# Turning the query order of the exponentials, so that one DMA stores a unit's result, in a hashed-attention and feed-forward kernel

## The chip, the cores and the metric

The kernel runs on one core of a Trainium2 chip. The metric is the device time of one execution in microseconds (us). Single executions of the same kernel scatter by up to 1.6% here (the kernel before: 303.5 to 308.3 us over its fast runs), so differences of less than that are read from several rounds and an interval, never from one run. One run of the kernel before, 308.87 us, counted as slow and is left out. One profiled execution of each kernel gives the trace.

TensorE does the matmuls, ScalarE the exponentials, VectorE and GpSimd other work on elements, and SyncE (SP) issues most transfers. SBUF is the working memory on the chip, PSUM the memory into which the matmuls write their sums. The granted clock is the share of its full clock that TensorE was given.

## The reference

```python
# attention over (4, 8, 768, 64): only pairs in the same hash bucket count
q_bucket, k_bucket = bits(q @ proj > 0), bits(k @ proj > 0)          # 6 bits
scores = where(q_bucket == k_bucket, q @ k.T / sqrt(64), -1e9)
attn = softmax(scores)
x = (attn @ v) as (batch, seq, 8 * 64)
# feed-forward on rows of x
xn = (x - mean) / sqrt(var + 1e-6) * g_ln
out = x + relu(xn @ w_ch1) @ w_ch2                                   # 512 -> 2048 -> 512
# [cut: shapes, the drawing of the inputs]
```

## The kernel before

The work goes in 12 units of 256 queries, three to a batch. A unit has six steps; a step makes scores (four heads, 256 keys, 256 queries) on TensorE into two PSUM tiles, two exponentials on ScalarE take them to bf16 in SBUF, and later matmuls use these tiles as weights against the values. The order of every instruction on every engine is fixed by one long word list.

```python
KJ, CC, TT = 6, 4, 32
out_view = [out[b].rearrange("(tt c u qt) d -> u c tt qt d", tt=TT, c=CC, u=3) for b in range(B)]

def S_(eng, s, h):        # scores: 24 matmuls a step, into two PSUM tiles [128, 2, 512] fp32
    # [cut]

def E_(eng, s, h):        # two of these a step; E is [128, 4, 512] bf16 in SBUF
    nc.scalar.activation(E(s)[:, heads(h)], sc(s, h), AF.Exp, scale=EXP_SCALE, bias=bias_sb)

def A_(eng, s, h):        # E as weights: 128 adjacent columns become 128 output partitions
    # [cut: loops]
    nc.tensor.matmul(acc[...], E(s)[:, i, 256 * kk + P * qt : 256 * kk + P * qt + P], vaug(...), ...)

def O_(eng, u, *a):       # the result of unit u: x is [128, 2, 512] fp32
    # [cut: which t, c, half]
    eng.dma_start(
        out=out_view[u // 3][u % 3][c][:, t, half(h)], in_=xt(u)[32 * c : 32 * c + 32, t, half(h)],
    )
```

A block of 128 queries lies in the order (c, t), c of 4 and t of 32, because the transposes on VectorE (L246, 72 of them in the trace), with the views of the kernel's `turn`, leave it so. The result therefore has partition 32c + t, while the row in DRAM goes with 4t + c, and a unit needs four stores of 32 partitions.

The softmax here doesn't subtract the row's maximum and nothing guards it: scores larger than these inputs give would overflow.

Of the kernel before, what the change touches and what calls it, by code (L numbers as in the profile page):

```python
# [590 lines left out]
```

## Time and profile before

| Kernel before | value |
|---|---|
| time, first three runs | 304.38, 305.44, 308.29 us |
| span of the profiled run | 303.0 us |
| TensorE busy | 292.2 us, 96% |
| ScalarE busy | 194.6 us, 64%, of it 153.1 us in 144 exponentials |
| stores | 56 (50 on SP's queue, 6 on ACT's) |

The lines themselves stand in the prediction. They are to be read from the busiest engine outwards: TensorE is nearly never idle (192.32 of 195.00 us busy from 75 to 270 us), ScalarE waits for TensorE (39.9 us for scores there), and the stores hold a queue for which no wait of TensorE is listed there.

### The profile page before, as it was taken

Reading aid. Unit: us, or ns where it says so; the run is one execution under the profiler, and the core shown is the slowest. Engines: PE = TensorE matmul, PEld = TensorE weight load, DVE = VectorE, ACT = ScalarE, POOL = GpSimd, SP = SyncE. Lnnn points to the kernel's source line nnn. Section 1 sums busy time; section 2 is a strip of 40 time slices with the busy share of each in tenths; the row PEclk is TensorE's granted clock in tenths of the full one; section 3 lists DMA queues with packets and bytes.
Section 4 is the critical chain, followed back from the end, with each engine's and each line's share of the span. In section 5 each row is a group of like instructions: output and inputs, shape, how many; then the busy total and the mean of one; then the engine's idle time right before and its main releaser. Section 6 shows DMA issues by size and latency. Waiting matters only on the chain.

```text
span 303.0 us, 9838 instructions
## 1 busy us (share of the span) xinstructions
PE 292.2 (96%) x4319; PEld 204.8 (68%) x4360; DVE 169.7 (56%) x348; ACT 194.6 (64%) x215; POOL 72.0 (24%) x112
## 2 busy tenths in 40 slices
PE   8999899999999999999999999999999999999994
PEld 7667676676666667676667677776657667685673
DVE  4678878378258527766345767555217446266012
ACT  2977789667667788686567676557666767561320
POOL 2792500211771005041600520911000101001000
PEclk9999999999999999999999999999999999999999
DMA  6999996937255265516306100310502102403122
GB/s 202 381 340 306 209 205 142 268 111 169 47 147 122 61 217 167 94 74 160 73 2 175 38 8 8 75 42 19 89 2 71 37 2 19 105 4 74 30 71 69
DMA packets 30426, 33.58 MB, mean 111 GB/s; under 512 B 15536, under 2 KB 27056, under 8 KB 30384
## 3 DMA queue, kind: packets, MB, share of 16 engines
...
HBM read 27.53 MB, written 6.29 MB: 112 GB/s over the span
## 4 chain that ended last, share of the span: by engine, by line
PE 80%; DMA 6%; SPq 6%; DVE 3%; issue 2%; ACT 1%; DVEq 0%; ACTq 0%
PE f L511 26%; PE sc L443 15%; PE acc L458 10%; DMA X<-in_q_dram 4%; SPq L420 3%; PE hp L408 3%; DMA xnT<-xc 3%; ACT E L449 1%; SPq L294 1%; PE f_100None L527 1%; PE f_101None L527 1%; PE f L527 1%; PE f_11None L527 1%; PE f_51None L527 1%; PE f_80None L527 1%
## 5 line engine op out<-in xcount | busy, mean ns | idle before, releaser
L449 ACT ACTIVATE E<-sc,bias_sb 128x1024 bf16<-128x1024 f32 x144 | 153.1, 1111 | 49.5 <-PE sc L443 48.3
L511 PE MATMUL f<-xnT,w_sb 128*128 128x256 bf16 x768 | 99.3, 273 | 0.8 <-DMA xnT<-xc 0.7
L511 PEld LDWEIGHTS <-w_sb 128*128 128x128 bf16 x768 | 70.9, 98 | 23.5 <-issue 7.9
L519 ACT ACTIVATE hb<-f 128x512 bf16<-128x512 f32 x57 | 33.9, 597 | 44.6 <-PE f L511 44.5
L527 PEld LDWEIGHTS <-hb 128*128 128x128 bf16 x400 | 37.7, 98 | 34.5 <-issue 2.7
L521 DVE TENSOR_SCALAR hb<-f 128x512 bf16<-128x512 f32 x39 | 26.9, 690 | 46.7 <-PE f L511 46.4
L443 PE MATMUL sc<-qb,kb 32*128 32x256 bf16 x1152 | 52.2, 267 | 0.0
L458 PEld LDWEIGHTS <-E 128*128 128x128 bf16 x1152 | 40.0, 98 | 6.5 <-issue 3.8
L458 PE MATMUL acc<-vaug,E 128*128 128x65 bf16 x1152 | 43.4, 194 | 0.1
L443 PE MATMUL sc<-G 6*128 6x256 bf16 x576 | 41.7, 273 | 0.9 <-DVE G L249 0.3
L489 POOL TENSOR_SCALAR rs<-mv 128x2 f32<-128x2 f32 x12 | 7.1, 595 | 104.6 <-DVE mv L483 104.3
L443 PEld LDWEIGHTS <-kb 32*128 32x128 bf16 x1152 | 30.2, 93 | 1.6
L443 PEld LDWEIGHTS <-G 6*128 6x128 bf16 x576 | 15.2, 91 | 18.8 <-issue 15.6
L246 DVE STREAM_TRANSPOSE T<-X 128x384 f32<-128x384 f32 x48 | 24.8, 554 | 3.4 <-PE hp L408 1.4
L469 DVE SCALAR_TENSOR_TENSOR acc<-vsB,acc 128x520 f32<-128x520 f32 x24 | 16.8, 701 | 15.3 <-PE acc L458 15.0
L356 POOL TENSOR_TENSOR t<-vn 128x256 f32<-128x256 f32 x18 | 12.9, 727 | 35.0 <-DMA out_dram<-x 18.0
L346 POOL CAST vaug<-vn 128x768 bf16<-128x768 f32 x16 | 13.1, 831 | 25.9 <-DMA G<-B 12.7
L484 DVE SCALAR_TENSOR_TENSOR xc<-x,mv,gB 128x512 bf16<-128x512 f32 x24 | 18.6, 776 | 0.8
L480 DVE BATCH_NORM_STATS2 st<-x 128x6 f32<-128x256 f32 x48 | 18.0, 417 | 0.7
L476 DVE TENSOR_TENSOR x<-acc,rc 128x512 f32<-128x512 f32 x24 | 16.6, 691 | 0.8
L257 POOL CAST kb<-T 128x768 bf16<-128x768 f32 x10 | 8.4, 842 | 30.2 <-DVE T L246 30.2
L315 PE MATMUL hf<-tp,pfull 128*128 128x256 f32 x48 | 13.2, 401 | 0.6 <-DVE tp L246 0.5
...
## 6 DMA issues: line engine op xcount, KB each, us to landing
...
G<-B SPq DMA_DIRECT2D x96, 4.5 KB
...
```

The lines of the kernel that those rows point to most:

```text
L246: nc.vector.transpose(d[:, j], s[:, j, kj0 : kj0 + n])
L443: nc.tensor.matmul(sc(s, i // 2)[:, i % 2, 256 * kk : 256 * kk + 256], lh, rh, start=(rep == 0), stop=(rep == 2), skip_group_check=True,)
L449: nc.scalar.activation(E(s)[:, heads(h)], sc(s, h), AF.Exp, scale=EXP_SCALE, bias=bias_sb)
L458: nc.tensor.matmul(acc[:, qt, (D + 1) * i : (D + 1) * (i + 1)], E(s)[:, i, 256 * kk + P * qt : 256 * kk + P * qt + P], vaug(u // 3)[:, 4 * ...
L469: nc.vector.scalar_tensor_tensor(acc, vs, EPS_ROW, acc, op0=AOP.mult, op1=AOP.add)
L476: nc.vector.tensor_tensor(xo, a[:, :, :, 0:D], rc.to_broadcast([P, 2, 4, D]), op=AOP.mult)
L480: nc.vector.bn_stats(stats(u)[:, qt, g], xt(u)[:, qt, 256 * g : 256 * g + 256])
L484: nc.vector.scalar_tensor_tensor(xc(u)[:, t], xt(u)[:, t], mv(u)[:, t, 0:1], gB, op0=AOP.subtract, op1=AOP.mult,)
L511: nc.tensor.matmul(f1[:, n].rearrange("p (t x) -> p t x", t=2), w1_sb[:, dt, P * nt : P * nt + P], xnT(u)[:, :, dt], start=(dt == 0), stop ...
L519: nc.scalar.activation(hb(u)[:, 2 * p : 2 * p + 2], f1, AF.Relu)
L521: eng.tensor_scalar_max(hb(u)[:, 2 * p : 2 * p + 2], f1, 0.0)
L527: nc.tensor.matmul(f2, hb(u)[:, nt, P * t : P * t + P], w2_sb[:, nt, half(h)], start=(nt == 0), stop=(nt == NNT - 1),)
```

## The change

Its intent: if the exponentials write each block of queries in the order (t, c), partition 4t + c comes out by itself, and a unit's 128 partitions go to DRAM in one store. Batch 0 keeps the old way.

```diff
+    U_TURNED = 3
+    out_turned = [out[b].rearrange("(p u qt) d -> u p qt d", u=3, qt=2) for b in range(B)]
 ...
     def E_(eng, s, h):
-        nc.scalar.activation(E(s)[:, heads(h)], sc(s, h), AF.Exp, scale=EXP_SCALE, bias=bias_sb)
+        dst, src = E(s)[:, heads(h)], sc(s, h)
+        if s // 6 >= U_TURNED:
+            dst = dst.rearrange("p i (n t c) -> p (i n) c t", t=TT, c=CC)
+            src = src.rearrange("p i (n c t) -> p (i n) c t", t=TT, c=CC)
+        nc.scalar.activation(dst, src, AF.Exp, scale=EXP_SCALE, bias=bias_sb)
 ...
+        elif u < NU - 1:
+            eng.dma_start(out=out_turned[u // 3][u % 3], in_=xt(u))
+        else:
+            r = slice(64 * c, 64 * c + 64)
+            eng.dma_start(out=out_turned[u // 3][u % 3][r, t, half(h)], in_=xt(u)[r, t, half(h)])
 ... [cut: the word list loses 30 stores and keeps every other word in its place]
```

The source is read straight; the destination steps by 4 bf16 elements, 8 bytes, in runs of 32. The last unit goes out in six stores of 64 partitions, on two queues.

More of the change, by code (lines that the diff above doesn't have):

```diff
@@ L71 @@
 na.v.5.1 nb.v.5.1 nc.v.5.1 ce.v.5.1 fl.s.5.1 cv.p.3.4.2 ce.v.5.0 fl.s.5.0 S.t.36.2 E.a.36.1 E.a.36.0 F.t.4.1 R.a.4.1
-cv.p.2.4.0 D.t.3.1.1 D.t.3.1.2 D.t.3.1.3 Z.v.3.1 O.s.3.2 O.s.3.1 sa.p.2.4.2 mo.s.2.1.2.3 A.t.36.2 F.t.4.7 R.a.4.7
-S.t.38.2 E.a.38.1 F.t.4.4 R.v.4.4 D.t.4.0.0 D.t.4.0.1 E.a.38.0 S.t.42.2 F.t.5.4 R.v.5.4 D.t.4.0.2 D.t.4.0.3 Z.v.4.0
+cv.p.2.4.0 D.t.3.1.1 D.t.3.1.2 D.t.3.1.3 Z.v.3.1 O.s.3.2 sa.p.2.4.2 mo.s.2.1.2.3 A.t.36.2 F.t.4.7 R.a.4.7 S.t.38.2
+E.a.38.1 F.t.4.4 R.v.4.4 D.t.4.0.0 D.t.4.0.1 E.a.38.0 S.t.42.2 F.t.5.4 R.v.5.4 D.t.4.0.2 D.t.4.0.3 Z.v.4.0
@@ L74 @@
 sa.p.2.4.1 F.t.5.3 R.v.5.3 mo.s.2.1.3.3 A.t.38.2 on.p.3 E.a.42.0 sa.p.2.4.0 E.a.42.1 S.t.39.2 E.a.39.1 E.a.39.0
-sp.t.2.0 sc.v.2.0 D.t.4.1.0 O.s.3.3 A.t.37.2 na.v.6.0 nb.v.6.0 nc.v.6.0 F.t.5.6 R.a.5.6 S.t.41.2 E.a.41.0 E.a.41.1
-D.t.4.1.1 D.t.4.1.2 D.t.4.1.3 Z.v.4.1 O.s.4.1 O.s.4.0 O.s.4.2 O.s.3.0 F.t.5.2 R.a.5.2 S.t.40.2 E.a.40.0 F.t.5.0
-R.v.5.0 cv.p.2.4.2 A.t.41.2 lv.s.3.0.1 A.t.39.2 lv.s.3.0.2 F.t.5.1 sb.p.2.4 su.p.2.4 E.a.40.1 S.t.44.2 E.a.44.1
-E.a.44.0 lv.s.3.0.0 A.t.40.2 lv.s.3.0.3 sa.p.3.0.1 R.v.5.1 sp.t.2.4 sc.v.2.4 D.t.5.0.0 F.t.5.7 R.a.5.7 S.t.46.2
@@ L79 @@
-E.a.46.0 E.a.46.1 na.v.6.1 nb.v.6.1 A.t.44.2 nc.v.6.1 ce.v.6.1 fl.s.6.1 ce.v.6.0 rs.p.6 F.t.5.5 D.t.5.0.1 S.t.43.2
-E.a.43.1 E.a.43.0 rs.p.5 fl.s.6.0 R.v.5.5 hm.t.3.0 tu.v.3.1.0.2 tu.v.3.1.1.2 bt.v.3.0 mo.s.3.0.0.1 mo.s.3.0.1.1
-mo.s.3.0.0.2 mo.s.3.0.2.2 mo.s.3.0.2.1 mo.s.3.0.0.0 mo.s.3.0.2.0 tu.v.3.1.1.3 mo.s.3.0.3.1 tu.v.3.1.1.1 tu.v.3.1.0.3
-mo.s.3.0.0.3 mo.s.3.0.3.2 D.t.5.0.2 D.t.5.0.3 S.t.47.2 E.a.47.0 E.a.47.1 F.t.6.3 R.v.6.3 A.t.42.2 A.t.43.2
-mo.s.3.0.1.2 Z.v.5.0 mo.s.3.0.1.0 CA.p.3.1.1.1 cv.p.3.0.0 F.t.6.1 R.a.6.1 S.t.45.2 E.a.45.1 E.a.45.0 D.t.5.1.0
@@ L84 @@
-D.t.5.1.1 F.t.6.6 R.a.6.6 na.v.7.0 S.t.48.2 E.a.48.1 nb.v.7.0 A.t.46.2 tu.v.3.1.1.0 A.t.45.2 mo.s.3.0.3.3
-CA.v.3.1.0.1 tu.v.3.1.0.0 sa.p.3.0.0 sb.p.3.0 mo.s.3.0.2.3 tu.v.3.1.0.1 hm.t.3.1 bt.v.3.1 mo.s.3.1.0.1 mo.s.3.1.1.3
-mo.s.3.1.2.2 mo.s.3.1.1.2 mo.s.3.0.3.0 E.a.48.0 S.t.50.2 E.a.50.0 E.a.50.1 nc.v.7.0 F.t.6.4 R.v.6.4 mo.s.3.1.1.1
-A.t.47.2 na.v.7.1 nb.v.7.1 nc.v.7.1 D.t.5.1.2 D.t.5.1.3 mo.s.3.1.2.1 ce.v.7.1 fl.s.7.1 cv.p.3.0.2 S.t.49.2 E.a.49.0
-F.t.6.0 R.v.6.0 E.a.49.1 A.t.48.2 A.t.50.2 ce.v.7.0 fl.s.7.0 rs.p.7 F.t.6.2 R.a.6.2 O.s.4.3 mo.s.3.1.1.0 Z.v.5.1
@@ L89 @@
-O.s.5.1 mo.s.3.1.0.2 S.t.53.2 E.a.53.0 E.a.53.1 CA.v.3.1.0.0 CA.p.3.1.1.0 mo.s.3.1.3.2 F.t.6.5 R.v.6.5 mo.s.3.1.3.1
-D.t.6.0.0 D.t.6.0.1 mo.s.3.1.2.3 F.t.6.7 R.v.6.7 mo.s.3.1.2.0 O.s.5.3 S.t.51.2 E.a.51.0 E.a.51.1 A.t.49.2 na.v.8.0
-F.t.7.0 R.a.7.0 D.t.6.0.2 D.t.6.0.3 Z.v.6.0 F.t.7.6 R.a.7.6 mo.s.3.1.0.0 S.t.52.2 E.a.52.1 F.t.7.5 mo.s.3.0.1.3
-nb.v.8.0 A.t.53.2 A.t.51.2 nc.v.8.0 O.s.5.2 R.v.7.5 F.t.7.1 R.v.7.1 E.a.52.0 A.t.52.2 na.v.8.1 nb.v.8.1 nc.v.8.1
-ce.v.8.1 fl.s.8.1 S.t.54.2 E.a.54.0 sa.p.3.0.2 su.p.3.0 sp.t.3.0 sc.a.3.0 sa.p.3.4.2 sa.p.3.4.0 sa.p.3.4.1
@@ L94 @@
-mo.s.3.1.0.3 D.t.6.1.0 D.t.6.1.1 mo.s.3.1.3.3 E.a.54.1 mo.s.3.1.3.0 F.t.7.7 R.a.7.7 S.t.56.2 E.a.56.0 E.a.56.1
-F.t.7.3 R.v.7.3 A.t.54.2 D.t.6.1.2 F.t.7.4 R.a.7.4 cv.p.3.4.0 S.t.55.2 E.a.55.1 E.a.55.0 A.t.56.2 F.t.7.2 R.a.7.2
-D.t.6.1.3 S.t.58.2 E.a.58.1 ce.v.8.0 fl.s.8.0 F.t.8.3 Z.v.6.1 O.s.6.1 O.s.6.2 D.t.7.0.0 D.t.7.0.1 R.v.8.3 sb.p.3.4
-su.p.3.4 sp.t.3.4 sc.v.3.4 E.a.58.0 S.t.57.2 E.a.57.1 E.a.57.0 O.s.5.0 F.t.8.1 R.v.8.1 D.t.7.0.2 D.t.7.0.3 O.s.6.0
-F.t.8.2 R.a.8.2 S.t.59.2 E.a.59.1 A.t.55.2 E.a.59.0 Z.v.7.0 D.t.7.1.0 D.t.7.1.1 D.t.7.1.2 D.t.7.1.3 Z.v.7.1 O.s.7.2
@@ L99 @@
-O.s.7.0 rs.p.8 O.s.7.1 F.t.8.0 R.a.8.0 O.s.6.3 S.t.61.2 E.a.61.0 E.a.61.1 F.t.8.5 R.a.8.5 na.v.9.0 nb.v.9.0 nc.v.9.0
-A.t.59.2 A.t.58.2 A.t.57.2 na.v.9.1 nb.v.9.1 nc.v.9.1 ce.v.9.0 S.t.63.2 E.a.63.0 E.a.63.1 fl.s.9.0 D.t.8.0.0
-D.t.8.0.1 F.t.8.4 R.a.8.4 S.t.62.2 E.a.62.0 E.a.62.1 ce.v.9.1 rs.p.9 fl.s.9.1 F.t.8.6 R.v.8.6 D.t.8.0.2 F.t.8.7
-R.a.8.7 S.t.65.2 E.a.65.1 E.a.65.0 D.t.8.0.3 Z.v.8.0 F.t.9.3 R.v.9.3 A.t.61.2 S.t.60.2 E.a.60.0 E.a.60.1 A.t.62.2
-F.t.9.0 R.v.9.0 D.t.8.1.0 S.t.64.2 E.a.64.0 E.a.64.1 F.t.9.5 R.v.9.5 A.t.60.2 D.t.8.1.1 F.t.9.6 R.a.9.6 S.t.68.2
@@ L104 @@
-E.a.68.1 E.a.68.0 na.v.10.0 nb.v.10.0 A.t.64.2 nc.v.10.0 A.t.63.2 A.t.65.2 na.v.10.1 nb.v.10.1 nc.v.10.1 ce.v.10.0
-ce.v.10.1 rs.p.10 fl.s.10.0 fl.s.10.1 F.t.9.7 R.a.9.7 S.t.67.2 E.a.67.1 F.t.9.4 R.a.9.4 D.t.8.1.2 D.t.8.1.3 E.a.67.0
-F.t.9.1 R.a.9.1 S.t.66.2 E.a.66.1 E.a.66.0 F.t.9.2 Z.v.8.1 O.s.8.0 D.t.9.0.0 O.s.8.2 A.t.67.2 tab.a O.s.8.1 O.s.8.3
-S.t.71.2 E.a.71.1 E.a.71.0 R.v.9.2 F.t.10.6 R.v.10.6 D.t.9.0.1 D.t.9.0.2 D.t.9.0.3 Z.v.9.0 S.t.69.2 E.a.69.1
-E.a.69.0 F.t.10.0 R.v.10.0 A.t.66.2 A.t.68.2 na.v.11.0 nb.v.11.0 nc.v.11.0 F.t.10.3 O.s.7.3 R.a.10.3 S.t.70.2
@@ L109 @@
-E.a.70.0 F.t.10.4 R.v.10.4 A.t.69.2 A.t.71.2 F.t.10.2 R.v.10.2 E.a.70.1 A.t.70.2 na.v.11.1 nb.v.11.1 nc.v.11.1
-ce.v.11.0 D.t.9.1.0 F.t.10.1 R.a.10.1 D.t.9.1.1 D.t.9.1.2 fl.s.11.0 F.t.10.5 R.a.10.5 D.t.9.1.3 F.t.10.7 ce.v.11.1
-rs.p.11 fl.s.11.1 Z.v.9.1 D.t.10.1.0 O.s.9.2 O.s.9.0 O.s.9.1 D.t.10.1.1 O.s.9.3 D.t.10.1.2 R.v.10.7 F.t.11.0
-D.t.10.1.3 R.a.11.0 F.t.11.4 R.a.11.4 Z.v.10.1 D.t.10.0.0 F.t.11.2 R.a.11.2 D.t.10.0.1 F.t.11.3 D.t.10.0.2 R.a.11.3
-F.t.11.1 R.a.11.1 D.t.10.0.3 Z.v.10.0 O.s.10.1 O.s.10.3 O.s.10.2 O.s.10.0 F.t.11.6 R.v.11.6 D.t.11.1.0.1 D.t.11.0.0
@@ L114 @@
-F.t.11.5 R.a.11.5 D.t.11.0.1 F.t.11.7 R.a.11.7 D.t.11.1.1.1 D.t.11.1.2.1 D.t.11.1.3.1 Z.v.11.1.1 O.a.11.1.1.1
-O.s.11.1.2.1 O.a.11.1.0.1 O.s.11.1.3.1 D.t.11.0.2 D.t.11.0.3 Z.v.11.0 O.s.11.0.3 O.a.11.0.1 O.s.11.0.0 O.a.11.0.2
-D.t.11.1.0.0 D.t.11.1.1.0 D.t.11.1.2.0 D.t.11.1.3.0 Z.v.11.1.0 O.s.11.1.1.0 O.a.11.1.3.0 O.a.11.1.2.0 O.s.11.1.0.0
+sp.t.2.0 sc.v.2.0 D.t.4.1.0 A.t.37.2 na.v.6.0 nb.v.6.0 nc.v.6.0 F.t.5.6 R.a.5.6 S.t.41.2 E.a.41.0 E.a.41.1 D.t.4.1.1
+D.t.4.1.2 D.t.4.1.3 Z.v.4.1 O.s.4.1 F.t.5.2 R.a.5.2 S.t.40.2 E.a.40.0 F.t.5.0 R.v.5.0 cv.p.2.4.2 A.t.41.2 lv.s.3.0.1
@@ new lines @@
+A.t.39.2 lv.s.3.0.2 F.t.5.1 sb.p.2.4 su.p.2.4 E.a.40.1 S.t.44.2 E.a.44.1 E.a.44.0 lv.s.3.0.0 A.t.40.2 lv.s.3.0.3
+sa.p.3.0.1 R.v.5.1 sp.t.2.4 sc.v.2.4 D.t.5.0.0 F.t.5.7 R.a.5.7 S.t.46.2 E.a.46.0 E.a.46.1 na.v.6.1 nb.v.6.1 A.t.44.2
+nc.v.6.1 ce.v.6.1 fl.s.6.1 ce.v.6.0 rs.p.6 F.t.5.5 D.t.5.0.1 S.t.43.2 E.a.43.1 E.a.43.0 rs.p.5 fl.s.6.0 R.v.5.5
+hm.t.3.0 tu.v.3.1.0.2 tu.v.3.1.1.2 bt.v.3.0 mo.s.3.0.0.1 mo.s.3.0.1.1 mo.s.3.0.0.2 mo.s.3.0.2.2 mo.s.3.0.2.1
+mo.s.3.0.0.0 mo.s.3.0.2.0 tu.v.3.1.1.3 mo.s.3.0.3.1 tu.v.3.1.1.1 tu.v.3.1.0.3 mo.s.3.0.0.3 mo.s.3.0.3.2 D.t.5.0.2
@@ new lines @@
+D.t.5.0.3 S.t.47.2 E.a.47.0 E.a.47.1 F.t.6.3 R.v.6.3 A.t.42.2 A.t.43.2 mo.s.3.0.1.2 Z.v.5.0 mo.s.3.0.1.0
+CA.p.3.1.1.1 cv.p.3.0.0 F.t.6.1 R.a.6.1 S.t.45.2 E.a.45.1 E.a.45.0 D.t.5.1.0 D.t.5.1.1 F.t.6.6 R.a.6.6 na.v.7.0
+S.t.48.2 E.a.48.1 nb.v.7.0 A.t.46.2 tu.v.3.1.1.0 A.t.45.2 mo.s.3.0.3.3 CA.v.3.1.0.1 tu.v.3.1.0.0 sa.p.3.0.0 sb.p.3.0
+mo.s.3.0.2.3 tu.v.3.1.0.1 hm.t.3.1 bt.v.3.1 mo.s.3.1.0.1 mo.s.3.1.1.3 mo.s.3.1.2.2 mo.s.3.1.1.2 mo.s.3.0.3.0
+E.a.48.0 S.t.50.2 E.a.50.0 E.a.50.1 nc.v.7.0 F.t.6.4 R.v.6.4 mo.s.3.1.1.1 A.t.47.2 na.v.7.1 nb.v.7.1 nc.v.7.1
@@ new lines @@
+D.t.5.1.2 D.t.5.1.3 mo.s.3.1.2.1 ce.v.7.1 fl.s.7.1 cv.p.3.0.2 S.t.49.2 E.a.49.0 F.t.6.0 R.v.6.0 E.a.49.1 A.t.48.2
+A.t.50.2 ce.v.7.0 fl.s.7.0 rs.p.7 F.t.6.2 R.a.6.2 mo.s.3.1.1.0 Z.v.5.1 O.s.5.1 mo.s.3.1.0.2 S.t.53.2 E.a.53.0
+E.a.53.1 CA.v.3.1.0.0 CA.p.3.1.1.0 mo.s.3.1.3.2 F.t.6.5 R.v.6.5 mo.s.3.1.3.1 D.t.6.0.0 D.t.6.0.1 mo.s.3.1.2.3
+F.t.6.7 R.v.6.7 mo.s.3.1.2.0 S.t.51.2 E.a.51.0 E.a.51.1 A.t.49.2 na.v.8.0 F.t.7.0 R.a.7.0 D.t.6.0.2 D.t.6.0.3
+Z.v.6.0 F.t.7.6 R.a.7.6 mo.s.3.1.0.0 S.t.52.2 E.a.52.1 F.t.7.5 mo.s.3.0.1.3 nb.v.8.0 A.t.53.2 A.t.51.2 nc.v.8.0
@@ new lines @@
+R.v.7.5 F.t.7.1 R.v.7.1 E.a.52.0 A.t.52.2 na.v.8.1 nb.v.8.1 nc.v.8.1 ce.v.8.1 fl.s.8.1 S.t.54.2 E.a.54.0 sa.p.3.0.2
+su.p.3.0 sp.t.3.0 sc.a.3.0 sa.p.3.4.2 sa.p.3.4.0 sa.p.3.4.1 mo.s.3.1.0.3 D.t.6.1.0 D.t.6.1.1 mo.s.3.1.3.3 E.a.54.1
+mo.s.3.1.3.0 F.t.7.7 R.a.7.7 S.t.56.2 E.a.56.0 E.a.56.1 F.t.7.3 R.v.7.3 A.t.54.2 D.t.6.1.2 F.t.7.4 R.a.7.4
+cv.p.3.4.0 S.t.55.2 E.a.55.1 E.a.55.0 A.t.56.2 F.t.7.2 R.a.7.2 D.t.6.1.3 S.t.58.2 E.a.58.1 ce.v.8.0 fl.s.8.0 F.t.8.3
+Z.v.6.1 O.s.6.1 D.t.7.0.0 D.t.7.0.1 R.v.8.3 sb.p.3.4 su.p.3.4 sp.t.3.4 sc.v.3.4 E.a.58.0 S.t.57.2 E.a.57.1 E.a.57.0
@@ new lines @@
+F.t.8.1 R.v.8.1 D.t.7.0.2 D.t.7.0.3 F.t.8.2 R.a.8.2 S.t.59.2 E.a.59.1 A.t.55.2 E.a.59.0 Z.v.7.0 D.t.7.1.0 D.t.7.1.1
+D.t.7.1.2 D.t.7.1.3 Z.v.7.1 O.s.7.2 rs.p.8 F.t.8.0 R.a.8.0 S.t.61.2 E.a.61.0 E.a.61.1 F.t.8.5 R.a.8.5 na.v.9.0
+nb.v.9.0 nc.v.9.0 A.t.59.2 A.t.58.2 A.t.57.2 na.v.9.1 nb.v.9.1 nc.v.9.1 ce.v.9.0 S.t.63.2 E.a.63.0 E.a.63.1 fl.s.9.0
+D.t.8.0.0 D.t.8.0.1 F.t.8.4 R.a.8.4 S.t.62.2 E.a.62.0 E.a.62.1 ce.v.9.1 rs.p.9 fl.s.9.1 F.t.8.6 R.v.8.6 D.t.8.0.2
+F.t.8.7 R.a.8.7 S.t.65.2 E.a.65.1 E.a.65.0 D.t.8.0.3 Z.v.8.0 F.t.9.3 R.v.9.3 A.t.61.2 S.t.60.2 E.a.60.0 E.a.60.1
@@ new lines @@
+A.t.62.2 F.t.9.0 R.v.9.0 D.t.8.1.0 S.t.64.2 E.a.64.0 E.a.64.1 F.t.9.5 R.v.9.5 A.t.60.2 D.t.8.1.1 F.t.9.6 R.a.9.6
+S.t.68.2 E.a.68.1 E.a.68.0 na.v.10.0 nb.v.10.0 A.t.64.2 nc.v.10.0 A.t.63.2 A.t.65.2 na.v.10.1 nb.v.10.1 nc.v.10.1
+ce.v.10.0 ce.v.10.1 rs.p.10 fl.s.10.0 fl.s.10.1 F.t.9.7 R.a.9.7 S.t.67.2 E.a.67.1 F.t.9.4 R.a.9.4 D.t.8.1.2
+D.t.8.1.3 E.a.67.0 F.t.9.1 R.a.9.1 S.t.66.2 E.a.66.1 E.a.66.0 F.t.9.2 Z.v.8.1 O.s.8.0 D.t.9.0.0 A.t.67.2 tab.a
+S.t.71.2 E.a.71.1 E.a.71.0 R.v.9.2 F.t.10.6 R.v.10.6 D.t.9.0.1 D.t.9.0.2 D.t.9.0.3 Z.v.9.0 S.t.69.2 E.a.69.1
@@ new lines @@
+E.a.69.0 F.t.10.0 R.v.10.0 A.t.66.2 A.t.68.2 na.v.11.0 nb.v.11.0 nc.v.11.0 F.t.10.3 R.a.10.3 S.t.70.2 E.a.70.0
+F.t.10.4 R.v.10.4 A.t.69.2 A.t.71.2 F.t.10.2 R.v.10.2 E.a.70.1 A.t.70.2 na.v.11.1 nb.v.11.1 nc.v.11.1 ce.v.11.0
+D.t.9.1.0 F.t.10.1 R.a.10.1 D.t.9.1.1 D.t.9.1.2 fl.s.11.0 F.t.10.5 R.a.10.5 D.t.9.1.3 F.t.10.7 ce.v.11.1 rs.p.11
+fl.s.11.1 Z.v.9.1 D.t.10.1.0 O.s.9.2 D.t.10.1.1 D.t.10.1.2 R.v.10.7 F.t.11.0 D.t.10.1.3 R.a.11.0 F.t.11.4 R.a.11.4
+Z.v.10.1 D.t.10.0.0 F.t.11.2 R.a.11.2 D.t.10.0.1 F.t.11.3 D.t.10.0.2 R.a.11.3 F.t.11.1 R.a.11.1 D.t.10.0.3 Z.v.10.0
@@ L117 @@
+O.s.10.1 F.t.11.6 R.v.11.6 D.t.11.1.0.1 D.t.11.0.0 F.t.11.5 R.a.11.5 D.t.11.0.1 F.t.11.7 R.a.11.7 D.t.11.1.1.1
+D.t.11.1.2.1 D.t.11.1.3.1 Z.v.11.1.1 O.s.11.1.0.1 O.a.11.1.1.1 D.t.11.0.2 D.t.11.0.3 Z.v.11.0 O.s.11.0.0 O.a.11.0.1
+D.t.11.1.0.0 D.t.11.1.1.0 D.t.11.1.2.0 D.t.11.1.3.0 Z.v.11.1.0 O.s.11.1.0.0 O.a.11.1.1.0
 """
@@ L544, in O_ @@
             t, c, h = slice(a[0], a[0] + 1), a[1], (a[2] if len(a) == 3 else None)
-        eng.dma_start(
-            out=out_view[u // 3][u % 3][c][:, t, half(h)], in_=xt(u)[32 * c : 32 * c + 32, t, half(h)],
-        )
+        if u < U_TURNED:
+            eng.dma_start(
+                out=out_view[u // 3][u % 3][c][:, t, half(h)], in_=xt(u)[32 * c : 32 * c + 32, t, half(h)],
+            )
+        elif u < NU - 1:
[3 more added lines that the diff above has]
+            eng.dma_start(out=out_turned[u // 3][u % 3][r, t, half(h)], in_=xt(u)[r, t, half(h)])
     OPS = dict(
```

## The prediction

The sum of the forecast below is 0 us for the exponentials, 0.1 us in the middle and 0.3 us at the end: 0.4 us of gain, with which 304.7 us were taken for the median after. The size of rival C was not shown, so that its 305 to 306 us, and its part in the 307 of the range, have no ground. The condition at which the prediction falls as a whole is that an exponential with the new write grows as the cast of k did, 1096 for 630 ns.

> **What bounds the kernel now.** I read the page's busy rows first, then the slices, then TensorE's waits in the long middle, then the exponentials and their neighbours, and the stores last. The busy rows of the page:
>
> ```profile
> span 303.0 us, 9838 instructions
> ...
> PE 292.2 (96%) x4319; PEld 204.8 (68%) x4360; DVE 169.7 (56%) x348; ACT 194.6 (64%) x215; POOL 72.0 (24%) x112
> ...
> PE   8999899999999999999999999999999999999994
> ...
> ACT  2977789667667788686567676557666767561320
> ...
> PEclk9999999999999999999999999999999999999999
> ```
>
> TensorE (PE) is busy for 292.2 of 303.0 us, 90% or more in almost every slice, at full clock. ScalarE (ACT) is second among the engines that the change touches, with 64%. So whatever isn't on TensorE counts only where TensorE waits for it. The stretch that holds nearly all exponentials of batches 1 to 3 is about 75 to 270 us; there, the windows view and the waits of TensorE and of ScalarE say:
>
> ```profile
> 75.00:270.00 195.00, 192.32 (x2995) 133.30 (x3025) 105.77 (x203) 134.13 (x148) 46.85 (x70) 1.00 0.30 73
> ...
> PE f L511 <- DMA xnT<-xc: 0.4, 1, 0.4
> PE f_20None L527 <- issue: 0.3, 2, 0.2
> ...
> ACT E L449 <- PE sc L443: 39.9, 51, 2.8
> ```
>
> The columns of the first line are the window, its length, and the busy time of PE, its weight loads, DVE, ACT and POOL. TensorE is idle for 195.00 - 192.32 = 2.7 us in 195, and the only wait for a transfer is one of 0.4 us for a transposed input of the feed-forward. No wait of TensorE for a store or for ScalarE is listed here. ScalarE waits for the scores, 39.9 us in 51 pieces: it follows TensorE, and not the other way round. Its idle time in the window is 195.00 - 134.13 = 60.9 us.
>
> The next lines are the group of the exponentials, and the source view of ScalarE's casts, which shows two casts of equal shape with different access orders:
>
> ```profile
> L449 ACT ACTIVATE E<-sc,bias_sb 128x1024 bf16<-128x1024 f32 x144 | 153.1, 1111 | 49.5 <-PE sc L443 48.3
> ...
> L253 ACT ACTIVATE kb<-tp x2: 1093/1096/1098, 7.8 to 9.2; 128x512 bf16<-128x512 f32 x2
> ...
> L253 ACT ACTIVATE qb<-tp x1: 630/630/630, 7.2 to 7.2; 128x512 bf16<-128x512 f32 x1
> ```
>
> An exponential takes 1.11 us, 144 of them. The cast of q goes straight through 512 elements and takes 630 ns; the cast of k reads its source at a stride of 32 fp32 elements (128 bytes) in runs of 4 and writes straight, and takes 1096 ns. So an access order can cost ScalarE 466 ns in 512 elements. This pair is the best evidence in the trace on the risky half of the change.
>
> The stores, and the end (the stores' source view, then the timeline of SP and of ACT's queue in the last microseconds):
>
> ```profile
> L545 SPq DMA_DIRECT2D out_dram<-x x50: 314/421/1231, 75.6 to 300.1; - x50
> L545 ACTq DMA_DIRECT2D out_dram<-x x6: 375/404/434, 296.3 to 300.1; - x6
> ...
> 299.73 0.78 SPq L545 DMA_DIRECT2D out_dram<-x  x2
> ...
> 299.73 0.85 ACTq L545 DMA_DIRECT2D out_dram<-x  x2
> ```
>
> An issue holds its queue for 0.42 us in the median. At the end, the last result is ready at 299.21 + 0.48 = 299.69 us; two stores go out on each of two queues, the later ones at 300.1, and the span ends at 303.0.
>
> [...]128 bytes between reads, and (1096 - 630) / 512 = 0.91 ns more per element[...]. No instruction of this trace shows ScalarE writing bf16 with an 8-byte step, which is what the change does. [...]
>
> **The change part by part.** (1) The 108 exponentials of units 3 to 11 (9 units of 6 steps of 2) still read the scores straight through, but write each block of 128 queries with a step of 4 elements, 8 bytes, in runs of 32. [...]I choose the reading that this costs nothing: 1.11 us each, 120 us for the 108, as before. The weight loads that read these tiles still read 128 adjacent columns, so TensorE's work is the same in number and size. Only the order of queries over the partitions changes, and nothing between the scores and the store depends on it.
>
> (2) Stores: before 56 (3 units of batch 0 with 4, 8 units with 4, the last unit with 12). After: 12 + 8 + 6 = 26. The 30 removed ones are 27 on SP and 3 on ACT's queue; at 0.42 us that is 11.3 us of SP's queue and 1.2 of ACT's. The bytes are the same, 512 KB a unit. In the word list of the schedule nothing else moves: every other operation keeps its place, and the kept store stands where the first of the four stood, right behind the sum that completes the unit. So SP waits for the same results as before, and only comes free 3 issues, 1.3 us, sooner after some of them. TensorE waits for what SP brings only once in the middle, 0.35 us at 215.84. Following it back, the transpose it waits for was issued at 211.38 behind three of the small mask copies (0.77 us each) and a transpose at 207.70 that itself started as soon as its input was ready. No store stands among them, so this wait stays. Sum for the middle: 11.3 us of issue time, none of it on the path; I allow 0 to 0.3 us.
>
> (3) The end. In each of the three last groups there is now one store per queue, over 64 partitions, where there were two over 32. The last issue starts at 299.73 instead of 300.1. Same bytes, same 2.5 us afterwards: 0.37 us saved[...]. I count 0.3.
>
> Sum: 0.3 at the end + 0.1 in the middle = 0.4 us of 303.0, or 0.1%. The runs before are 304.38, 305.44 and 308.29, so their median has more scatter in it than the whole gain; the profiled run had 304.76. I take 304.7 for the median after.
>
> **The rivals.** *A. The strided write costs what the strided read did.* Then each exponential grows by 0.91 ns x 1024 = 0.93 us, 108 of them by 100 us. The window's ScalarE would need 134 + 98 (105 instructions fall in it) = 232 us of 195, so ScalarE would bound it: at least 303 + 37 = 340 us, and with the latency of scores, exponential, next scores in each of the 54 steps (0.77 + 0.23 + 2 x 2.04 = 5.1 us against 195 / 54 = 3.6 now) up to 380. For it: the k cast. Against it: [...]the order was evidently chosen so that the large step falls on the narrow 2-byte side. I give it 6%.
>
> *B. The cost is per run, not per element.* The k cast has 512 / 4 = 128 runs; 466 / 128 = 3.6 ns a run. The new write has 1024 / 32 = 32 runs: +0.12 us an exponential, 12.6 us of ScalarE in all. This fits into the 60.9 us of idle time, but the schedule is tight in places: the exponentials that start at 257.64 last to 259.76, and the next scores, which need their banks, start at 259.82. A pair that is 0.23 us longer would stop TensorE there. If one in four of the 54 steps is as tight, the loss is 14 x 0.2 = 2.8 us; all of them, 12. So 305 to 317, most likely 308. I give it 8%.
>
> *C. The larger store is in the way.* A unit's 512 KB now goes out at once[...]. The transposes of a unit are mostly issued before the store, not after; one tight place is 275.50 to 278.00, when the last unit's transposes go out just ahead of a store, with the feed-forward that needs them starting at 280.56.[...] Against it: the DMA share is 0.30 in the middle. It would make 305 to 306.
>
> *D. SP's queue is a hidden bound,* and 11 us less of it lets everything move up. For it: the chain that ended last gives SPq 6%. Against it: the pieces of it lie before 51 us, in batch 0, whose stores do not change, and at 208 to 211 us among the mask copies. TensorE has only 2.7 us of idle time to give back in the window, so even all of it would be below 1%.
>
> **Range and chances.** [...]the time is 304 to 305.5; C and the scatter of single runs (308.29 among three) stretch that to 307; B adds a tail to 310; D goes down to 302.5. So the predicted time is 304.7 us, with 302.8 to 307.8 for 8 times in 10. Two per cent are 6.1 us. Faster would need over 6.1 us out of the 2.7 + 2.9 + start that TensorE doesn't fill: 0.02. Slower is A and the worse half of B: 0.09. Within 2%: 0.89.
>
> **What would show each step.** Right: the exponentials' group still has one mean near 1111 ns, and the source view no second population from about 82 us on; TensorE's busy time stays at 292 and its idle time in the window under 3 us; 26 stores; the last sum-up is followed by one issue per queue and the span ends some 2.9 - 0.1 us after the issue starts. Wrong: exponentials of about 2.0 us with ScalarE at over 95% in the middle (A), about 1.23 us with new waits of weight loads or scores for ScalarE (B), new waits of the feed-forward for transposes (C), or a TensorE idle time in the middle below 1 us (D).[...]

## The result, and the profile after

The changed kernel takes 427.64 us in the median of four runs (426.16 to 430.3); the kernel before had 305.73 in the four runs beside it. The ratio is 1.3983, with a 95% interval of 1.3868 to 1.4099. Ratios here are the mean time of one kernel's fast runs over that of the other's of the same rounds, so not quite the ratio of the medians. The change is 40% slower, and the prediction, with 302.8 to 307.8 us, was wrong.

The page of the changed kernel: busy time, slices, the chain that ended last by engine, and two groups (busy time, mean in ns, idle time before them and what ended it).

```profile
span 424.5 us, 9805 instructions
...
PE 325.6 (77%) x4319; PEld 221.1 (52%) x4360; DVE 169.9 (40%) x348; ACT 336.3 (79%) x215; POOL 72.5 (17%) x112
...
PE   8999998786567765687786667966787666887996
...
ACT  4878867988989888988888898879889989868121
...
PEclk9999999988998899988898989899899989868999
...
ACT 55%; PE 29%; issue 5%; SPq 4%; DMA 3%; DVE 2%; ACTq 0%; DVEq 0%
...
L454 ACT ACTIVATE E<-sc,bias_sb 128x1024 bf16<-128x1024 f32 x144 | 299.8, 2184 | 48.7 <-PE sc L444 47.6
...
L444 PE MATMUL sc<-G 6*128 6x256 bf16 x576 | 51.2, 282 | 77.7 <-ACT E L454 77.0
```

TensorE fell from 96% to 77% of a longer span, and ScalarE is busy in nearly every slice of the middle. The exponentials' mean went from 1111 to 2184 ns, though 36 of the 144 are unchanged. The chain went from 80% TensorE to 55% ScalarE. The scores group has 77.0 us of idle time in front of it that an exponential ended; before, none was listed. The granted clock, at 90% or more in every slice before, dips.

The exponentials by source line (shortest, median, longest in ns), then the window in which batches 1 to 3 now have nearly all their exponentials (106 of 108) (length, then PE, weight loads, DVE, ACT, POOL), and TensorE's longest wait in it (total, times, longest):

```profile
L454 ACT ACTIVATE E<-sc,bias_sb x144: 1102/2533/2583, 10.2 to 390.3; 128x1024 bf16<-128x1024 f32 x144
```

```profile
75.00:392.00 317.00, 228.49 (x3026) 151.81 (x3057) 106.50 (x204) 274.75 (x150) 47.80 (x70) 0.91 0.16 45
```

```profile
PE sc L444 <- ACT E L454: 75.8, 46, 2.6
```

There are two populations: 1.1 us in batch 0 and about 2.53 us afterwards. From the group's total, (299.8 - 36 x 1.111) / 108 = 2.41 us of busy time each, because two neighbours overlap by about 0.25 us. From 75 us to about the last exponential it was 195 us and is 317 us now, which is the whole loss: 122 of 424.5 - 303.0 = 121.5 us. ScalarE has 274.75 busy us in it and TensorE 228.49, so neither is full. The chain in order of time shows why (start, length, what):

```profile
202.66 4.82 ACT E L454 x2
...
207.53 0.93 PE sc L444 x24
208.45 0.16 issue
...
220.33 4.82 ACT E L454 x2
...
225.20 0.89 PE sc L444 x24
226.09 4.80 ACT E L454 x2
```

Two exponentials, then the next scores, then exponentials again. The scores need the PSUM tiles that the exponentials still read (the 46 waits above, 75.8 us), and the exponentials need the scores, so the two engines take turns: 5.76 us from the pair at 220.33 to the one at 226.09. Most of the stretch looks like this; in a few steps, as after 208.45, the chain goes through the feed-forward before it comes back. 54 steps of 5.76 us would be 311 of the 317 us. Before, the pair took 2.12 us and TensorE filled the time between with the feed-forward; now TensorE waits for exponentials 46 times in this stretch.

### The profile page after: what moved, and what is told of

The parts are those of the page before. It is cut to its first block, busy times and chain, and to the rows that moved or that the text cites. A ratio compares the mean times of both kernels' runs of the same rounds, so it can differ in the third digit from the quotient of the medians.

```text
span 424.5 us, 9805 instructions
## 1 busy us (share of the span) xinstructions
PE 325.6 (77%) x4319; PEld 221.1 (52%) x4360; DVE 169.9 (40%) x348; ACT 336.3 (79%) x215; POOL 72.5 (17%) x112
## 4 chain that ended last, share of the span: by engine, by line
ACT 55%; PE 29%; issue 5%; SPq 4%; DMA 3%; DVE 2%; ACTq 0%; DVEq 0%
ACT E L454 54%; PE sc L444 13%; PE f L516 6%; DMA X<-in_q_dram 3%; SPq L421 2%; PE acc L463 1%; PE f_41None L532 1%; DMA xnT<-xc 1%; SPq L295 1%; PE f_90None L532 1%; PE f_100None L532 1%; PE f_101None L532 1%; PE f L532 1%; PE f_110None L532 1%; PE f_91None L532 1%
## 5 line engine op out<-in xcount | busy, mean ns | idle before, releaser
L454 ACT ACTIVATE E<-sc,bias_sb 128x1024 bf16<-128x1024 f32 x144 | 299.8, 2184 | 48.7 <-PE sc L444 47.6
L516 PE MATMUL f<-xnT,w_sb 128*128 128x256 bf16 x768 | 107.7, 288 | 7.1 <-ACT hb L524 5.6
L444 PE MATMUL sc<-G 6*128 6x256 bf16 x576 | 51.2, 282 | 77.7 <-ACT E L454 77.0
L516 PEld LDWEIGHTS <-w_sb 128*128 128x128 bf16 x768 | 74.5, 102 | 35.4 <-issue 18.1
L444 PEld LDWEIGHTS <-G 6*128 6x128 bf16 x576 | 22.6, 93 | 98.9 <-issue 93.9
L532 PEld LDWEIGHTS <-hb 128*128 128x128 bf16 x400 | 40.7, 105 | 43.2 <-issue 15.7
L444 PE MATMUL sc<-qb,kb 32*128 32x256 bf16 x1152 | 59.3, 282 | 0.0
L524 ACT ACTIVATE hb<-f 128x512 bf16<-128x512 f32 x57 | 36.7, 646 | 25.2 <-PE f L516 25.1
L463 PE MATMUL acc<-vaug,E 128*128 128x65 bf16 x1152 | 46.0, 198 | 3.5 <-ACT E L454 3.4
L444 PEld LDWEIGHTS <-kb 32*128 32x128 bf16 x1152 | 35.0, 97 | 1.1
```

The lines of the kernel that those rows point to most:

```text
L444: nc.tensor.matmul(sc(s, i // 2)[:, i % 2, 256 * kk : 256 * kk + 256], lh, rh, start=(rep == 0), stop=(rep == 2), skip_group_check=True,)
L454: nc.scalar.activation(dst, src, AF.Exp, scale=EXP_SCALE, bias=bias_sb)
L463: nc.tensor.matmul(acc[:, qt, (D + 1) * i : (D + 1) * (i + 1)], E(s)[:, i, 256 * kk + P * qt : 256 * kk + P * qt + P], vaug(u // 3)[:, 4 * ...
L516: nc.tensor.matmul(f1[:, n].rearrange("p (t x) -> p t x", t=2), w1_sb[:, dt, P * nt : P * nt + P], xnT(u)[:, :, dt], start=(dt == 0), stop ...
L524: nc.scalar.activation(hb(u)[:, 2 * p : 2 * p + 2], f1, AF.Relu)
L532: nc.tensor.matmul(f2, hb(u)[:, nt, P * t : P * t + P], w2_sb[:, nt, half(h)], start=(nt == 0), stop=(nt == NNT - 1),)
```

## The experiments

The standing theory is that **the loss is the longer exponentials alone (theory 1)**; the rival is that the **larger stores, the new row order or the clock carry a part (rival 2)**. Below that is the question why an 8-byte step costs so much.

### The stores alone

```diff
-        if s // 6 >= U_TURNED:
+        if False:
```

> The changed kernel with the exponentials writing straight, as before: only the stores are changed (26 instead of 56), so the rows of batches 1 to 3 land in another order, wrong on purpose. Theory 1 (the whole loss is the exponentials' write order): 0.2 to 0.8 us under the kernel before, exponentials at 1.11 us, granted clock 1.00. Rival 2 (the larger stores get in the way of the transposes, the mask copies or the clock): clearly above 306 us, and a part of the 121 us shows here.

It gave 305.73 us against 304.5 for the kernel before: ratio 1.0048, interval 1.0014 to 1.0083; rows in the wrong order as intended. By the interval the stores carry at most 0.8% of the time, 2.5 of the 121 us. But the small gain that was expected isn't there either: the interval lies just above 1. (The kernel that turns by the read, below, has the same stores and 1.0008, so a loss of half a per cent isn't certain.) The last issues, of SP's and of ACT's queue:

```profile
299.34 0.47 SPq L558 DMA_DIRECT2D out_dram<-x  x1
299.35 0.50 ACTq L558 DMA_DIRECT2D out_dram<-x  x1
```

Each now takes about 0.5 us instead of 0.39 to 0.43, and the span of 302.6 us ends 3.26 us after the first of them starts. In the kernel before, with two issues on each queue, the span ended 3.27 us after 299.73. The time to the end is the same within the 0.1 us to which spans are given. What took up the saved issue was not shown.

### The exponentials alone

```diff
+        if s // 6 >= 3:
+            dst = dst.rearrange("p i (n t c) -> p (i n) c t", t=TT, c=CC)
+            src = src.rearrange("p i (n c t) -> p (i n) c t", t=TT, c=CC)
 ...
-            out=out_view[u // 3][u % 3][c][:, t, half(h)], in_=...
+            # units 3 to 11: the turned view, rows 32c to 32c + 32; four stores as before
```

> The kernel before with the changed write order of the 108 exponentials, and four stores of 32 partitions to a unit as before, to the right rows: correct result. Theory 1: the whole loss, 424 to 431 us, with 108 exponentials near 2.53 us. Rival 2: well below, and the difference is the stores'.

Correct, 426.62 us, ratio 1.4015 (1.3962 to 1.4067): the whole loss, with the old number of stores.

```profile
span 425.1 us, 9879 instructions
...
L453 ACT ACTIVATE E<-sc,bias_sb 128x1024 bf16<-128x1024 f32 x144 | 299.9, 2185 | 50.1 <-PE sc L443 48.9
```

### A table of walks

Each unit of batches 1 to 3 walked its exponentials in another order (the step of the write, or of the read, or the order of the runs); each order has its own line number.

```diff
+        elif u == 3: nc.scalar.activation(wr(dst, 2), rd(src, 2), AF.Exp, **k)    # write steps 2, 4, 8, 16
+        elif u == 8: nc.scalar.activation(walk(dst, 4), walk(src, 4), AF.Exp, **k)  # runs of 4, jumps on both sides
+        elif u == 9: ...  # scores read at a step of 32 fp32, straight write
 ... [cut]
```

Theory 1b says that the cost grows with the bytes of the write's step.

> A table: the kernel before, and in each unit of batches 1 to 3 the exponentials walk their tiles in another order, wrong on purpose; only the durations count. Step of the bf16 write 2, 4, 8, 16 elements (4, 8, 16, 32 bytes) in runs of 32 with a straight read; then runs of 32 and of 4 that read and write step 1 but jump from run to run on both sides; then a read of the scores at a step of 32 fp32 in runs of 32 x 4 with a straight write; then reads at a step of 2 and 4 fp32 (8 and 16 bytes) with a straight write. Theory 1a (any step over one 2-byte element breaks up the write, a cost per element): steps 2, 4, 8 and 16 all near 2.5 us, runs of 32 near 1.11. Theory 1b[...]: step 2 clearly cheaper than step 4, steps 8 and 16 dearer. Rival B of the prediction (a cost per run): runs of 32 near 2.5 us, runs of 4 far over. For the reads no theory has a number; the cast of k suggests 2.0 us for the step of 32.

In the lines below, 463 is straight, 465, 467, 469 and 471 are write steps of 2, 4, 8 and 16 elements, 475 jumps in runs of 4 on both sides, and 477 reads the scores at a step of 128 bytes and writes straight:

```profile
L469 ACT ACTIVATE E<-sc,bias_sb 128x1024 bf16<-128x1024 f32 x12 | 56.4, 4903 | 6.5 <-PE sc L443 6.5
L471 ACT ACTIVATE E<-sc,bias_sb 128x1024 bf16<-128x1024 f32 x12 | 53.3, 4679 | 8.1 <-PE sc L443 8.1
L463 ACT ACTIVATE E<-sc,bias_sb 128x1024 bf16<-128x1024 f32 x36 | 38.0, 1111 | 9.0 <-PE sc L443 7.9 <-PE acc L491 1.1
...
L467 ACT ACTIVATE E<-sc,bias_sb 128x1024 bf16<-128x1024 f32 x12 | 29.0, 2544 | 4.1 <-PE sc L443 4.1
L465 ACT ACTIVATE E<-sc,bias_sb 128x1024 bf16<-128x1024 f32 x12 | 16.2, 1397 | 4.7 <-PE sc L443 4.7
L477 ACT ACTIVATE E<-sc,bias_sb 128x1024 bf16<-128x1024 f32 x12 | 12.8, 1113 | 5.0 <-PE sc L443 5.0
...
L475 ACT ACTIVATE E<-sc,bias_sb 128x1024 bf16<-128x1024 f32 x12 | 12.7, 1111 | 6.0 <-PE sc L443 6.0
```

After the first bar stand the busy time in us and the mean of one in ns. Straight: 1111 ns. Write steps of 4, 8, 16 and 32 bytes: 1397, 2544, 4903 and 4679. Runs, jumps and reads from PSUM cost nothing: 1111 and 1113, and reads at 8 and 16 bytes, not shown, 1111 and 1112. (The 2.0 us that the cast of k had suggested for the read at 128 bytes were wrong; that cast, 1096 for 630 ns, reads SBUF.) So rival B of the prediction (a cost per run) falls. Theory 1a, in which any broken-up write costs the same, falls too: the cost follows the bytes of the step up to 16 and then stays. Theory 1b fits so far: less 0.25 us of fixed time (an estimate: what makes 8 bytes just twice as dear as 4), the steps of 4, 8, 16 and 32 bytes take 1.12, 2.24, 4.5 and 4.3 ns per element: in proportion to the bytes up to 16, and about 4.5 ns there.

### The turn made by VectorE

```diff
         d = dst.rearrange("p j (kj c t) -> p j kj c t", c=CC, t=32)
+        if q:      # queries of batches 1 to 3; the exponentials write straight again
+            d = dst.rearrange("p j (kj t c) -> p j kj c t", c=CC, t=32)
 ... [cut: the call that sets q, and the exponentials' write as before]
```

> The intent of the change by another road: the exponentials write straight, and the 24 VectorE transposes of the queries of batches 1 to 3 write with a step of 4 fp32 instead, so that queries and their bits are in the new order from the start; the 26 stores of the changed kernel; correct result. Theory 1: as fast as the kernel before or up to 1 us faster, if the transposes (0.55 us straight) don't grow beyond about 1.5 us, which VectorE's idle time takes up. If VectorE pays per element as ScalarE did, they grow to about 1.1 us, 13 us of VectorE in all, mostly hidden: 303.5 to 307 us.

Correct, 305.72 us, ratio 1.0048 (1.0003 to 1.0093). The same row order and the same stores as in the changed kernel cost half a per cent, 0.9% at most by the interval, when the order is made elsewhere. The transposes (shortest, median, longest), before and now, show the price that VectorE hides:

```profile
L246 DVE STREAM_TRANSPOSE T<-X x48: 534/558/580, 19.5 to 178.8; 128x384 f32<-128x384 f32 x48
...
L249 DVE STREAM_TRANSPOSE T<-X x48: 525/699/884, 21.0 to 182.1; 128x384 f32<-128x384 f32 x48
```

In the second line half of them write fp32 at 16 bytes.

A third road, to load the exponentials' tiles as weights in the turned order, was not run.

### The turn made by the exponentials' read

```diff
-            dst = dst.rearrange("p i (n t c) -> p (i n) c t", t=TT, c=CC)
-            src = src.rearrange("p i (n c t) -> p (i n) c t", t=TT, c=CC)
+            dst = dst.rearrange("p i (n t c) -> p (i n) t c", t=TT, c=CC)
+            src = src.rearrange("p i (n c t) -> p (i n) t c", t=TT, c=CC)
```

> The changed kernel, 26 stores, with the permutation of the exponentials moved from the write to the read: they take the scores at a step of 32 fp32 in runs of 4 and write the same bytes to the same places in straight order. Correct result. Theory 1 (ScalarE's write side alone is to blame; the table showed 1.11 us for this walk): 304 to 306 us, within 0.5% of the kernel before, exponentials at 1.11 us, clock 1.00. Rival (the order of the walk as such, or the new order of rows further on): well above 310 us.

```profile
span 302.6 us, 9805 instructions
...
L454 ACT ACTIVATE E<-sc,bias_sb 128x1024 bf16<-128x1024 f32 x144 | 153.0, 1111 | 49.6 <-PE sc L444 48.4
```

Correct, 305.52 us against 304.93, ratio 1.0008 (0.9961 to 1.0056), clock 0.998 to 1.000. The same elements go to the same places; only which side jumps has changed. This is the changed kernel without its loss. It doesn't beat the kernel before: the stores were never on the path.

### A smaller step: how much does the schedule hide?

```diff
-            dst = dst.rearrange("p i (n t c) -> p (i n) c t", t=TT, c=CC)     # step of 4
+            dst = dst.rearrange("p i (n t c) -> p (i n) c t", t=32, c=2)      # step of 2, wrong on purpose
 ... [cut: src in the same way]
```

> The changed kernel with a write step of 2 elements instead of 4 (1.40 us an exponential in the table), wrong on purpose. It measures how much growth the schedule hides. If ScalarE's total decides (31 us more in a window with 61 us idle): within 1% of the kernel before. If it is the loop scores, exponential pair, next scores: 0.29 us x 108 = 31 us growth, of which the 121 us lost for 1.42 x 108 = 154 us suggest that some 33 us are hidden: 303 to 315 us, with new waits of the scores for exponentials.

314.25 us, ratio 1.0295 (1.0234 to 1.0355), clock 1.00. ScalarE's busy time rose by 221.8 - 194.6 = 27.2 us, and about 9 of them came out as time. New waits of the scores for exponentials appear, short ones:

```profile
PE sc L444 <- ACT E L454: 5.2, 16, 0.5
```

This is what the loop explanation had forecast (303 to 315 us with new waits of the scores), and the idle time of ScalarE in the window, 60.9 us, was not the room that there was.

### Held as long, without a strided write

```diff
+        if s // 6 >= U_TURNED:      # on top of the kernel that turns by the read
+            nc.scalar.activation(spare, sc(s, h), AF.Exp, scale=EXP_SCALE, bias=bias_sb)
         nc.scalar.activation(dst, src, AF.Exp, scale=EXP_SCALE, bias=bias_sb)
```

> The kernel with the strided read, and each of the 108 exponentials preceded by a second one into a spare tile, straight: ScalarE is held for about 2.1 us for each, in place of 2.53, without any strided write. Correct result. Theory 1 (nothing but the time for which ScalarE is held counts): growth of 1.0 us less the hidden 0.3 us, times 108: 370 to 390 us, and the granted clock falls as in the changed kernel, to 0.91 to 0.95[...]. Rival (strided writes also disturb something else, the weight loads or the clock): under 350 us or clock 1.00.

387.58 us, ratio 1.2706 (1.2604 to 1.2809), correct. The time is as expected; the clock, 0.961 to 0.978, fell less than the 0.91 to 0.95 expected. The two groups of exponentials, and TensorE's longest wait:

```profile
L457 ACT ACTIVATE E<-sc,bias_sb 128x1024 bf16<-128x1024 f32 x144 | 158.7, 1117 | 10.2 <-PE sc L444 9.1
L456 ACT ACTIVATE spare<-sc,bias_sb 128x1024 bf16<-128x1024 f32 x108 | 120.7, 1118 | 33.5 <-PE sc L444 33.5
```

```profile
PE sc L444 <- ACT E L457: 58.2, 45, 2.0
```

Every exponential writes straight, and yet the same wait stands there with 58.2 us. A second kernel added a third straight one, of 384 elements:

```diff
+            nc.scalar.activation(spare[:, 0, :384], sc(s, h)[:, 0, :384], AF.Exp, scale=EXP_SCALE, bias=bias_sb)
```

> The kernel with the doubled straight exponentials and a third of 384 elements into the spare tile, so that ScalarE is held for about 2.4 us for each of the 108, as long as the strided pair holds it in the changed kernel (4.8 us a pair), again without a strided write. Correct result. Theory 1 (only the time counts): 420 to 430 us. Rival (the strided writes also cost TensorE or its clock something): under 418 us, with a granted clock well above the 0.92 to 0.935 of the changed kernel.

This expectation was missed: 459.74 us, ratio 1.5057 (1.4977 to 1.5137). The aim was a pair of 4.8 us; the trace has this pair, first and last instruction:

```profile
205.58 1.11 ACT L456 ACTIVATE spare<-sc,bias_sb 128x1024 bf16<-128x1024 f32 x1 [0.28 <-PE sc L444]
...
209.83 1.11 ACT L458 ACTIVATE E<-sc,bias_sb 128x1024 bf16<-128x1024 f32 x1
```

From 205.58 to 209.83 + 1.11 are 5.36 us, because the small one took 0.58 us, more than I had reckoned. Against the time that a pair holds ScalarE, the points still rise in order: 2.12 us gives 305, 4.12 us (twice) 388, 4.82 us (the changed kernel) 427, 5.36 us 460. The changed kernel, the only one of them with strided writes, lies on the line of its two neighbours: from 388 to 460 are 72 us for 1.24 us of pair, 58 us for one, so 4.82 us should give 388 + 0.70 x 58 = 429. So no harm of strided writes is seen in the time besides how long they hold ScalarE. (A small one is in the trace: the feed-forward's relus on ScalarE take 676 ns in the median with strided exponentials among them, 597 before and in this last kernel.) And the clock falls furthest here, without any:

```profile
span 459.3 us, 10063 instructions
...
PEclk9999998898977888898977988999799879877999
```

### Why 8 bytes are dear

An extra copy of 384 elements after each exponential, to or from spare tiles; only durations count.

```diff
+        elif u == 4: nc.scalar.activation(wr(f32a, 2), rd(src, 2), AF.Copy)      # fp32 at 8 bytes
+        elif u == 7: nc.scalar.activation(wr(b16a, 4), rd(src, 4), AF.Copy)      # bf16 at 8 bytes
 ... [cut: straight ones, fp32 at 16 bytes, reads from SBUF, two on VectorE]
```

The 4.47 ns for a step of 16 bytes, and half of them for 8, are the estimate from the table of walks; theory 1b was taken to hold for any type and function.

> The kernel before with one extra instruction of 384 elements after each exponential of batches 1 to 3, into spare tiles; correct result, only the extra durations count. ScalarE copies from the scores: fp32 straight, fp32 at a step of 2 (8 bytes), fp32 at a step of 4 (16 bytes), bf16 straight, bf16 at a step of 4 (8 bytes); from SBUF fp32 at steps of 2 and 4 (8 and 16 bytes) to straight bf16; VectorE copies to bf16, straight and at a step of 4. Theory 1b[...]: fp32 at 8 bytes 2.24 ns per element (some 0.5 us more than straight), at 16 bytes 4.47 ns (1.4 us more), bf16 at 8 bytes 0.55 us more. Rival (it is 2-byte writes alone): fp32 steps near the straight time. For the reads from SBUF: the cast of k had 0.91 ns more per element at 128 bytes. VectorE: no number from theory 1; the transposes grew by about a half at 16 bytes.

Below, 466 and 468 write fp32 at 8 and 16 bytes, 472 bf16 at 8 bytes on ScalarE, and 480 the same on VectorE, where 478 is straight:

```profile
L472 ACT ACTIVATE b16a<-sc 128x384 bf16<-128x384 f32 x12 | 12.3, 1026 | 0.0
L480 DVE CAST b16a<-sc 128x384 bf16<-128x384 f32 x12 | 12.1, 1011 | 12.8 <-ACT E L449 12.3
...
L468 ACT ACTIVATE f32a<-sc 128x384 f32<-128x384 f32 x12 | 10.4, 865 | 0.0
...
L478 DVE CAST b16a<-sc 128x384 bf16<-128x384 f32 x12 | 6.7, 557 | 12.8 <-ACT E L449 12.7
...
L466 ACT ACTIVATE f32a<-sc 128x384 f32<-128x384 f32 x12 | 6.2, 516 | 0.0
```

Theory 1b, which made no difference between the types, falls: at the same 8 bytes fp32 takes 516 ns, nearly the straight time (492), and bf16 1026, twice that. A second set tried groups of adjacent bf16:

```diff
+        if u == 3: nc.scalar.activation(wr(b16a, 2, 2), rd(src, 2, 2), AF.Copy)   # pairs at 8 bytes
+        elif u == 4: nc.scalar.activation(wr(b16a, 4, 2), rd(src, 4, 2), AF.Copy) # pairs at 16 bytes
 ... [cut: groups of four, single ones at 6, 8, 12 and 64 bytes, reads of bf16]
```

> The kernel before with one extra ScalarE copy of 384 elements after each exponential of batches 1 to 3, scores to a bf16 spare tile or spare to spare; only durations count (straight 0.50 us, single bf16 at 8 bytes 1.02, fp32 at 8 bytes 0.51, fp32 at 16 bytes 0.86 in the table before). Units in turn: pairs of adjacent bf16 at a step of 8 bytes, pairs at 16 bytes, groups of four at 16 bytes, single bf16 at 6, 12, 8 and 64 bytes, then bf16 read from SBUF at 8 and at 16 bytes with a straight write. Theory 2 (what is dear is a write of 2 bytes alone[...]): pairs at 8 bytes near 0.51, pairs at 16 bytes not over 0.86, groups of four at 16 bytes near 0.50, singles at 6 and 12 bytes near 0.82 and 1.5. Rival[...]: pairs at 8 bytes 0.62 (8 bytes spanned per pair, 192 pairs, 2.24 ns each, plus 0.19), pairs at 16 bytes 1.05, groups of four at 16 bytes 0.62, 64 bytes near 1.9. Reads of bf16: as reads of fp32 at equal bytes (0.55 and 0.89) or, if 2-byte reads are dearer too, over 1.0.

Here 464 is pairs at 8 bytes, 466 pairs at 16 bytes, 476 single elements at 64 bytes:

```profile
L476 ACT ACTIVATE b16a<-sc 128x384 bf16<-128x384 f32 x12 | 22.0, 1837 | 0.0
...
L466 ACT ACTIVATE b16a<-sc 128x384 bf16<-128x384 f32 x12 | 6.2, 516 | 0.0
...
L464 ACT ACTIVATE b16a<-sc 128x384 bf16<-128x384 f32 x12 | 5.9, 493 | 0.0
```

All ScalarE copies of the two sets, medians in ns:

| what | straight | 6 bytes | 8 bytes | 12 bytes | 16 bytes | 64 bytes |
|---|---|---|---|---|---|---|
| write fp32, from PSUM | 492 | | 514 | | 862 | |
| write bf16 singly, from PSUM | 500 | 824 | 1024 | 1448 | | 1839 |
| write bf16 in pairs, from PSUM | | | 492 | | 513 | |
| write bf16 in fours, from PSUM | | | | | 492 | |
| read fp32 from SBUF, write bf16 straight | | | 547 | | 885 | |
| read bf16 from SBUF, write bf16 straight | | | 544 | | 904 | |

No straight read from SBUF of this size was timed. Theory 2 holds in each of its numbers: two adjacent bf16 at a step of 8 or 16 bytes are about as cheap (492 and 513 ns) as a straight write (500), and lone 2-byte elements are dear at every step tried (824 to 1839). For these, the sum of theory 1b by the bytes of the step stays fair: from 8 to 12 bytes the copy grows by 424 ns for 384 x 4 bytes, 4.4 ns for 16 bytes. The same sum leaves 0.18 us fixed (an estimate); less that, the 1839 ns at 64 bytes are 4.3 ns for an element, as at 32 bytes in the table of walks, and 4 bytes at a step of 16 take 1.8 ns whether they are one fp32 (384 of them in 862 ns) or two bf16 (192 in 513 ns). Pairs at larger steps, and pairs that start on an odd element, were not tried. In VectorE's two copies the median went from 558 to 1010 ns, so it isn't ScalarE's alone. Why a lone bf16 is dearer these runs don't show; that stays open.

## Why the prediction was wrong

**The step that failed is part 1 of the sum**: "I choose the reading that this costs nothing: 1.11 us each." Measured: 2.53 us. The only test of a step in the trace was the cast of k, a read of fp32 at 128 bytes (1096 ns for 630); that a bf16 write at 8 bytes is free was the assumption, which no line of that trace shows. For fp32 at 8 bytes it is nearly so, for writes as for reads from SBUF (514 and 547 ns, against 492 and 500 for straight copies from PSUM); for lone bf16 it isn't (1024). The growth counted as 0 us was 108 x 1.42 = 153 us of summed durations and 142 of busy ScalarE time; the span grew by 121.5 us.

**Rival A had the mechanism and the wrong size.** It took 0.93 us more per exponential from the cast of k, where it was 1.42, and 340 to 380 us, where it was 427. Its loop is right: it said 5.1 us a step from pairs of 4.1, and the trace shows 5.76 from pairs of 4.82. The doubled straight exponentials, with pairs of 4.12, gave 388, near the 380 of that reckoning. The 6% were the error: the argument against it, that the large step falls on the narrow 2-byte side, was the wrong way round (at 8 bytes 1024 ns for bf16, 514 for fp32), and "no instruction of this trace shows ScalarE writing bf16 with an 8-byte step" should have kept the chance much higher. The pair of casts proved that order can make an instruction 1.7 times as long (1096 for 630 ns); that is no ground for calling another unseen order free.

**Rival B** named a cost that doesn't exist (runs of 4 and of 32: 1111 ns). Its reading of the schedule as tight was good: 0.29 us more per exponential cost 9 us.

**Part 2** held: 30 fewer stores gave nothing in the middle. **Part 3**, 0.3 us at the end, was mis-sized; it is 0.0 us to the 0.1 us of a span, as the time from the first of the last issues to the end stayed at 3.27 and 3.26 us. (Its 2.5 us after the last issue are 303.0 - 300.1 - 0.4 of the trace before.) **Rivals C and D** fell with the stores alone at 1.0048 of the time before. The sign that was named for D, TensorE idle below 1 us in the middle, does stand in that run's trace (195 - 194.59 = 0.41 us), but with no gain in time: TensorE's busy time over the run is higher too, 295.1 us for 292.2.

The granted clock was in no step. TensorE's work is slower at it (the feed-forward's matmul 288 ns in the mean at a clock of 0.935, 273 at 0.998), and as the scores are in the loop (mostly 0.85 to 0.93 us on the chain instead of 0.77), it adds a little to each step. It falls as the scores wait more for the exponentials: 1.00 in the kernel with the step of 2 (16 waits, 0.5 us at most, 5.2 in all), 0.96 to 0.98 in the doubled one (45, 2.0, 58.2), 0.916 to 0.935 in the changed one (47, 2.6, 77.0), 0.89 to 0.90 with the third exponential (49, 3.2, 88.8). Length, number and sum of the waits rise together here, so these runs don't say which of them counts; one lone wait of 1.8 us, in the kernel turned by VectorE, left its clock at 1.00. In stretches the granted clock was half: in this line of the changed kernel's trace (a stretch of 3.2 us) the third number from the end is the clock, 0.50.

```profile
181.60:184.80 3.20, 3.17 (x30) 2.10 (x31) 2.12 (x4) 2.74 (x3) 3.20 (x6) 0.50 0.25 46
```

Eight matmuls of the feed-forward that start in it, at 183.03, take 1.89 us; eight at 177.55, at a clock of 1.00, took 1.03. What makes the clock fall was not shown, and how much of the 121 us it makes was not separated.
